# Queries and keys of the last six pairs: a token per partition and a transposing DMA in place of transposes on TensorE

## The chip, the cores and the metric

The kernel runs on one core of a Trainium2 chip. The metric is the device time of one execution in microseconds (us), the median over several runs. Engines: PE (TensorE, matrix products), DVE (VectorE), ACT (ScalarE), POOL (GpSimd) and SP (SyncE). Here SP only issues DMAs; POOL issues DMAs and also does elementwise work, in one order with them.

## The reference

Attention with a causal sliding window of 64 tokens, over 8 batches, 8 heads, 576 tokens and a head size of 64, followed by a two-layer network with a hard-swish between the layers.

```python
scores = scale * np.matmul(q, k.transpose(0, 1, 3, 2))
mask = (rel >= 0) & (rel < window)          # rel = query position - key position, window = 64
attn = softmax(np.where(mask, scores, -1e9))
attn_out = np.matmul(attn, v)
x = attn_out.transpose(0, 2, 1, 3).reshape(4608, 512)
h = x @ w_in                                # 512 -> 2048
out = (h * np.clip(h + 3.0, 0.0, 6.0) / 6.0) @ w_out
```

Inputs and output are float32 in DRAM; the kernel computes in bf16 with float32 sums.

## The kernel before

**Pairs.** The unit of attention is a pair: two heads of one batch, on partitions 0 to 63 and 64 to 127. There are 32 pairs, t = 4b + g (batch b, pair g of the batch). Pairs 0 to 7 have paths of their own at the start; from pair 8 on, `group(t, n)` (L781) is called once for each pair.

**What a group holds.** In the order in which the instructions are issued: P.V of pair t (`pv`, L421); the turning of pair t + 2 (`turn`, L289: 9 pieces x 2 heads x 2 for queries and keys = 36 transposes of 64x64 on PE, into the two PSUM banks `tk` and `tq`); the scores of pair t + 1 (`s_first` L309, `s_rest` L323) and behind them the softmax weights (`weights`: exponentials on ACT, L332 and L336, then three multiplications with the window's 0/1 mask on POOL, L341 and L344); the division by the row sums (`pv_out`, on DVE); the copy of the turned keys from PSUM to `KT` on DVE (`turned(t + 2, 0)`, L296); the turning of the output into `xT` (`x_`, L465: two or three transposing DMAs on SP); two units of the two-layer network (`weave(2)`); the copy of the turned queries to `QT` on ACT (`turned(t + 2, 1)`, L296); and the remaining units of the network that this group is due (`weave(n - 2)`).

**The network.** A block is 512 tokens. A first-layer unit is four matmuls 128x128x512 into `hT` (L513), then L525 on ACT and L526 on DVE make `gT`; a second-layer unit is four matmuls into `acc` (L550), and after sixteen of them ACT copies (L556) and SP stores (L558). Units wait in the queue `moe` and are woven between the attention's steps.

**Order.** Every engine works in the order of issue (the order is written out by hand). An engine that waits holds up all that stands behind it on that engine; between engines there are only the waits on data and on buffers.

**Loads.** POOL issues them, and they turn float32 into bf16 on the way. `load_qk(b, n, first)` (L124, L128) loads n pairs with one DMA for the keys and one for the queries: 64 partitions, on each of them 9 consecutive tokens of a head in one run of 2304 bytes. Token 9p + r stands on partition p, so the 9 pieces of a head are transposed one by one, and the copies L296 put the tokens back in order. After groups 8 to 27 the last loop (L906 to L931) issues the loads of the next batch: from batch 3 on pairs 0 and 1 after its first group, V after the second, and after the third the shifted copy of V (`shift`, L167 and L168, on SP) and pairs 2 and 3.

**Buffers.** `KT` and `QT` are rings of four, indexed t % 4; keys have 64 zero columns in front. Scores read the keys of a window with a step of two (`keys`, L301).

Of the kernel before, what the change touches and what calls it, by code (L numbers as in the profile page):

```python
# [11 lines left out]
BF16 = mybir.dt.bfloat16  # L12
# [13 lines left out]
P = 128  # L26
D = 64
W = 64
R = 6
VC = 72  # L30
RL = 9
# [6 lines left out]
def kernel(  # L38
# [9 lines left out]
    nc = tc.nc  # L48
    B, H, S, _ = q.shape
    DM, FF = moe_w_in.shape  # L50
    NT = B * S
    NG = H // 2
    SP = S // R
    NW = S // W
    NM = (S + P - 1) // P
# [9 lines left out]
    stage = ctx.enter_context(tc.tile_pool(name="stage", bufs=2))  # L65
# [13 lines left out]
    def ring(n, shape, dtype, name):  # L79
        return [consts.tile(shape, dtype, name=f"{name}{i}") for i in range(n)]  # L80
# [1 line left out]
    win16 = consts.tile([P, NG, FF], BF16, name="win16")  # L82
    wout16 = consts.tile([P, NFC, DM], BF16, name="wout16")
    xT = consts.tile([P, NG, XR], BF16, name="xT")
    KT = ring(4, [P, W + S], BF16, "KT")
    QT = ring(4, [P, S], BF16, "QT")
    QZ = ring(4, [P, 2, W], BF16, "QZ")
    Vflat = ring(4, [P, NM * H * VC], BF16, "V")
    Vn, Vs = ([t[:].rearrange("p (m h c) -> p m h c", m=NM, h=H) for t in Vflat[i::2]] for i in range(2))
# [5 lines left out]
    Pw = [t[:].rearrange("p h m a w -> p (h m a w)").rearrange("p (h c m r w) -> p h c m r w", h=2, c=2, m=2, r=2) for t in Pz]  # L95
    P0 = ring(4, [D, 2, 2, W], BF16, "P0")
    halves = (slice(0, D), slice(D, P))


    def load_pair_0():  # L100
# [23 lines left out]
    def load_qk(b, n=NG, first=0):  # L124
        t = staged[b] if first else stage.tile([P, H, RL * D], BF16, name="qk9", tag="qk")
        hs = slice(2 * first, 2 * (first + n))
        for z, src in enumerate((k, q)):
            nc.gpsimd.dma_start(  # L128
                out=t[halves[z], hs], in_=src[b, hs].rearrange("h (p r) d -> p h (r d)", r=RL)
            )  # L130
        return t

    def load_early_v():
        for m in range(NM):
            n = min(P, S - m * P)
            nc.gpsimd.dma_start(
                out=Vn[0][:n, m, :, 0:D], in_=v[0, :, m * P : m * P + n, :].rearrange("h s d -> s h d"),
            )
# [49 lines left out]
    first = consts.tile([P, 2, W], BF16, name="first")  # L188
# [29 lines left out]
    def transposed_heads(pool, src, g):  # L218

        tp = pool.tile([P, R, SP], BF16, name="tp", tag="bk")  # L220
        for r in range(R):
            for h in range(2):
                nc.tensor.transpose(
                    out=tp[h * D : (h + 1) * D, r, :],
                    in_=src[:, 2 * g + h, r * D : (r + 1) * D], identity=ident[:SP, :SP],
                )
        return tp

    def t_q(t):
        b, g = divmod(t, NG)  # L230
        tp = transposed_heads(ps_h, staged[b][0], g)
        nc.scalar.copy(
            out=QT[t][:].rearrange("q (p r) -> q p r", r=R), in_=tp[:].rearrange("q r p -> q p r"),
        )

    def padded(t, move=nc.vector.tensor_copy):
        for h in range(2):
            move(out=QZ[t][halves[h], h], in_=QT[t][halves[h], S - W : S])

    def t_k(t):  # L240
        b, g = divmod(t, NG)
        tp = transposed_heads(ps_acc, staged[b][1], g)
        nc.vector.tensor_copy(
            out=KT[t % 4][:, W:].rearrange("q (p r) -> q p r", r=R),
            in_=tp[:].rearrange("q r p -> q p r"),
        )

    def s_early(t):

        kt, qt = KT[t], QT[t]  # L250
        sc = [ps_t.tile([P, NM - 1, 2, W], F32, name="sc", tag="bk") for _ in range(2)]
# [42 lines left out]

    def turned(t, z, on_vector=False):
        (nc.scalar.copy if z and not on_vector else nc.vector.tensor_copy)(  # L296
            out=(QT[t % 4][:] if z else KT[t % 4][:, W:]).rearrange("q (p r) -> q p r", r=RL),
            in_=hosts[t][z][:, 0:S].rearrange("q (r p) -> q p r", p=W),
        )

    def keys(t, h, k0, r):  # L301
        return KT[t % 4][halves[h], W + k0 + r : W + k0 + P : 2]

    def s_first(t, host):

        s = [x[0:D, 6 * P : 8 * P].bitcast(F32).rearrange("p (r w) -> p r w", w=W) for x in hosts[host]]
        for r in range(2):
            for h in range(2):
                nc.tensor.matmul(  # L309
                    s[h][:, r], lhsT=keys(t, h, 0, r), rhs=QT[t % 4][halves[h], 0:W], start=True, stop=True,  # L310
                )
        return s

    def s_rest(t):

        ss = [ps_t.tile([P, 2, 2, 2, W], F32, name="s", tag="bk") for _ in range(2)]
        for c in range(2):
            for m in range(2):
                for r in range(2):
                    for h in range(2):  # L320
                        for i in range(2):
                            w = 4 * m + 2 * i + 1 + c
                            nc.tensor.matmul(  # L323
                                ss[h][halves[i], c, m, r], lhsT=keys(t, h, W * (w - 1), r),
                                rhs=QT[t % 4][halves[h], w * W : (w + 1) * W], start=True, stop=True,
                            )
        return ss

# [271 lines left out]
    def weave(n):  # L600
        for _ in range(min(n, len(moe))):
            moe.popleft()()
# [18 lines left out]
    def s_max(t, fm):  # L621
        kt, qt, pw, p0 = KT[t % 4], QT[t % 4], Pw[t % 4], P0[t % 4]
        for w in range(S // W):
            k0 = W * max(w - 1, 0)
            sc = ps_t.tile([P, 2, P], F32, name="sm", tag="bk")
            se = fb.tile([P, 2, P], F32, name="se", tag="fs")
            for h in range(2):
                nc.tensor.matmul(
                    sc[0:W, 0], lhsT=qt[halves[h], w * W : (w + 1) * W],
                    rhs=kt[halves[h], W + k0 : W + k0 + P], start=True, stop=True,  # L630
                )
                nc.vector.tensor_tensor(
                    out=se[0:W, h], in0=sc[0:W, 0], in1=fm[0:W, min(w, 1)], op=ADD,
                )
            mx = fb.tile([P, 2], F32, name="mx")
            nc.vector.reduce_max(out=mx[0:W], in_=se[0:W], axis=mybir.AxisListType.X)
            nc.vector.tensor_tensor(
                out=se[0:W], in0=se[0:W], in1=mx[0:W].unsqueeze(2).to_broadcast([W, 2, P]), op=SUB,
            )
            pe = work.tile([P, 2, P], BF16, name="pe", tag="e0")  # L640
            nc.scalar.activation(out=pe[0:W], in_=se[0:W], func=EXP, scale=scale)
            c, j = (w - 1) % 2, (w - 1) // 2
            part = halves[j % 2 if w else 0]
            tp = ps_t.tile([P, 2, 2, W], BF16, name="pt", tag="bk")
            for h in range(2):
                for r in range(2):
                    nc.tensor.transpose(
                        out=tp[part, h, r], in_=pe[0:W, h, r:P:2], identity=ident[0:W, 0:W]
                    )
            nc.vector.tensor_copy(out=pw[part, :, c, j // 2] if w else p0[:], in_=tp[part])  # L650
# [36 lines left out]
    T = B * NG  # L687

    def warm(pool, n, cols=TB):
# [5 lines left out]
    staged = {}  # L695
# [6 lines left out]
        out=ident[:], in_=ident[:], pattern=[[-1, P]], compare_op=mybir.AluOpType.not_equal,  # L702
# [4 lines left out]
    window()  # L707
    for t in KT:
        nc.vector.memset(t[:, 0:W], 0.0)
# [21 lines left out]
    warm(ps_h, 4, W)  # L731
    t_k(0)
    t_q(0)
    padded(0)
    t_k(1)
# [45 lines left out]
    def group(t, n):  # L781

        if t >= 2 * NG:
            pv(t)
        if t + 2 < T:
            turn(t + 2)
        if t + 1 < T:
            host = t + 2
            opened(host)
            s = s_first(t + 1, host)  # L790
            weights(t + 1, s, s_rest(t + 1))
        if t >= 2 * NG:
            pv_out(t)
        if t + 2 < T:
            turned(t + 2, 0)
        if t >= 2 * NG:
            x_(t)
        weave(2)
        if t + 2 < T:
            turned(t + 2, 1)  # L800
        weave(n - 2)

    def turn_two(t):
# [14 lines left out]
    n = NG  # L818
# [12 lines left out]
    for t in range(n, n + 4):  # L831
        if t < n + 3:
            turn(t + 1)
        s = s_first(t, min(t + 1, n + 3))
# [71 lines left out]
    for t in range(2 * NG, T):  # L906
        b, g = divmod(t, NG)
        if g == 0 and b > 2:
            queue_block(b - 1, lead=4 if b == 3 else 2)
            if b == 3:  # L910
                arrange(2, (
                    -1, -2, 0, 1, 2, 3, -3, 4, 5, -4, 6, 7, 8, -5, 9, -6, 10, 11, 12, 13, -7,
                    14, 15, -9, -10, -8, -11, -12,
                ))
        group(t, shares[g] if b == 2 else -(-len(moe) // (NG - g)))
        if b == 2:
            if g == 0:
                load_v(3)
            if g == 1:
                shift(3)  # L920
            if g > 0:
                load_qk(3, 1, g)
        elif b + 1 < B:
            if g == 0:
                staged[b + 1] = load_qk(b + 1, 1)
                load_qk(b + 1, 1, 1)
            if g == 1:
                load_v(b + 1)
            if g == 2:
                shift(b + 1)  # L930
                load_qk(b + 1, 2, 2)  # L931
    late[0] = 2
    queue_last(NTB - 2)
    flag = flagged()
# [35 lines left out]
```

## Time and profile before

| what | value |
|---|---|
| median of 3 runs | 315.24 us (315.19 to 315.67) |
| profiled execution, its own time | 316.28 us |
| span of its instructions | 314.6 us |
| mean granted PE clock | 0.995 |
| DMA, mean | 114 GB/s |

The span runs from the first to the last instruction on the core; the rest of the execution's time lies around it. A page cuts the span into 40 slices of some 7.9 us, with the busy share of each engine in tenths. The chain of waits is followed back from the last instruction: at each step to what released it. In a timeline a row has its start (us from the start of the span), its length, the engine, the line, and the instruction; rows of SP and the DMA rows of POOL are the issue of a DMA and not its transfer. A row that stands for several instructions ends with their count.

### The profile page before, as it was taken

The page shows a single profiled execution, that of the slowest core. Times are in us where ns is not written, and L with a number is a line of the kernel's source. Part 1 is how long each engine was busy: PE and PEld are TensorE (multiplying, and loading weights), DVE is VectorE, ACT ScalarE, POOL GpSimd, SP SyncE. Part 2 cuts the span into 40 slices and gives each one's busy share as a digit, 9 for nine tenths or more (in the row PEclk, how much of TensorE's full clock was granted, in tenths as well). Part 3 has the DMA queues.
Part 4 walks back from the last instruction along what each step waited for, and adds up shares of the span by engine and source line. Part 5 has one row for each costly group of instructions (what it writes and reads, how often), then busy time and mean ns, then how long its engine had stood idle before and what let it go on. Part 6 is the DMA issues. An engine that isn't in the chain of part 4 may idle for free.

```text
span 314.6 us, 10707 instructions
## 1 busy us (share of the span) xinstructions
PE 299.5 (95%) x4565; PEld 151.0 (48%) x4608; DVE 180.4 (57%) x411; ACT 184.6 (59%) x350; POOL 131.3 (42%) x181
## 2 busy tenths in 40 slices
PE   7889989999999999999999999999999999999992
PEld 3454445555555554444555555555544444444440
DVE  7767647598547755773577447754776155344200
ACT  3838555877658656773677457754764266454410
POOL 8861404868887536653665366533330000000000
PEclk9999999999999999999999999999999999999998
DMA  8999995969996976697469744983021100100121
GB/s 155 167 205 200 198 192 123 220 119 100 205 144 102 144 167 114 76 132 188 84 83 139 169 109 79 131 193 88 19 56 52 69 33 0 70 34 33 36 82 60
DMA packets 57848, 35.96 MB, mean 114 GB/s; under 512 B 40128, under 2 KB 51904, under 8 KB 57792
## 3 DMA queue, kind: packets, MB, share of 16 engines
q0 software_dynamic: 35744, 18.52, 45.8%
q1 hardware_dynamic: 22048, 16.67, 21.0%
q8 instruction: 38, 0.62, 0.8%
q14 instruction: 18, 0.15, 0.1%
HBM read 37.62 MB, written 9.44 MB: 150 GB/s over the span
## 4 chain that ended last, share of the span: by engine, by line
PE 81%; DMA 9%; POOL 3%; DVE 3%; issue 2%; ACT 1%; POOLq 0%; ACTq 0%; DVEq 0%
PE acc L550 36%; PE hT L513 34%; DMA qk<-in_q_dram 7%; PE o L421 4%; PE s L323 3%; DMA V<-in_v_dram 2%; PE tk L289 2%; PE acco L550 1%; POOL qk L117 1%; PE tq L289 1%; DVE gT L526 1%; POOL qk L128 1%; POOL wout L179 1%; DVE opl L448 0%; DVE V L160 0%
## 5 line engine op out<-in xcount | busy, mean ns | idle before, releaser
L526 DVE SCALAR_TENSOR_TENSOR gT<-t,hT 128x512 bf16<-128x512 bf16 x141 | 95.7, 686 | 74.3 <-ACT t L525 73.2
L513 PE MATMUL hT<-xT,win 128*128 128x512 bf16 x548 | 131.5, 379 | 1.1 <-DVE gT L526 0.2
L550 PE MATMUL acc<-wout,gT 128*128 128x512 bf16 x522 | 126.7, 379 | 2.5 <-issue 1.1
L525 ACT ACTIVATE t<-hT,half_const 128x512 bf16<-128x512 f32 x141 | 95.6, 689 | 48.2 <-PE hT L513 46.3
L513 PEld LDWEIGHTS <-win 128*128 128x128 bf16 x576 | 55.3, 98 | 65.2 <-issue 0.4
L550 PEld LDWEIGHTS <-gT 128*128 128x128 bf16 x576 | 54.5, 98 | 64.2 <-issue 0.9
L344 POOL TENSOR_TENSOR Pz<-e,band 128x512 bf16<-128x512 bf16 x48 | 54.1, 1144 | 0.0
L341 POOL TENSOR_TENSOR P<-e,first 64x256 bf16<-64x256 bf16 x24 | 15.8, 660 | 74.4 <-ACT e L332 74.4
L556 ACT COPY osb<-acc 128x512 f32<-128x512 f32 x34 | 19.9, 586 | 42.0 <-PE acc L550 42.0
L336 ACT ACTIVATE e<-s 128x512 bf16<-128x512 f32 x56 | 30.1, 591 | 0.0
L296 DVE COPY KT<-tk 128x576 bf16<-128x576 bf16 x28 | 21.0, 749 | 6.9 <-ACT e L332 5.8
L147 POOL DMA_DIRECT2D V<-in_v_dram x22 | 18.0, 829 | 8.5 <-DMA wout<-in_moe_w_out_dram 5.6
L448 DVE TENSOR_TENSOR opl<-o,recs 128x256 bf16<-128x256 f32 x52 | 19.6, 419 | 0.5
L430 DVE TENSOR_REDUCE sums<-o 128x10 f32<-128x20 f32 x26 | 4.6, 175 | 23.9 <-PE o L421 23.8
L296 ACT COPY QT<-tq 128x576 bf16<-128x576 bf16 x27 | 17.2, 638 | 1.5 <-PE tq L289 1.5
L332 ACT ACTIVATE e<-tk 64x128 bf16<-64x128 f32 x28 | 7.6, 270 | 17.7 <-PE tq L309 17.7
L421 PEld LDWEIGHTS <-Pz 64*64 64x64 bf16 x1008 | 11.4, 108 | 10.7 <-issue 10.2
L289 PE MATMUL tk<-ident,qk 64*64 64x64 bf16 x504 | 14.3, 195 | 0.0
L289 PE MATMUL tq<-ident,qk 64*64 64x64 bf16 x504 | 14.0, 195 | 0.3 <-DMA qk<-in_q_dram 0.3
L128 POOL DMA_DIRECT2D qk<-in_k_dram x22 | 14.1, 640 | 0.3 <-issue 0.3
L323 PE MATMUL s<-QT,KT 64*64 64x64 bf16 x896 | 13.8, 194 | 0.0
L128 POOL DMA_DIRECT2D qk<-in_q_dram x22 | 13.8, 627 | 0.0
(106 smaller groups left out, 199.9 us busy)
## 6 DMA issues: line engine op xcount, KB each, us to landing
out_dram<-osb SPq DMA_DIRECT2D x36, 256.0 KB, 2.5
V<-in_v_dram POOLq DMA_DIRECT2D x16, 256.0 KB, 6.0
qk<-in_q_dram POOLq DMA_DIRECT2D x19, 144.0 KB, 4.5
qk<-in_k_dram POOLq DMA_DIRECT2D x19, 144.0 KB, 4.3
V<-V SPq DMA_DIRECT2D x6, 432.0 KB, 5.1
wout<-in_moe_w_out_dram POOLq DMA_DIRECT2D x2, 1024.0 KB, 17.4
qk<-in_k_dram POOLq DMA_DIRECT2D x6, 288.0 KB, 4.4
qk<-in_q_dram POOLq DMA_DIRECT2D x6, 288.0 KB, 5.6
```

The costliest lines, as they stand in the source:

```text
L128: nc.gpsimd.dma_start(out=t[halves[z], hs], in_=src[b, hs].rearrange("h (p r) d -> p h (r d)", r=RL))
L289: nc.tensor.transpose(out=hosts[t][z][halves[h], r * W : (r + 1) * W], in_=staged[b][halves[z], 2 * g + h, r * D : (r + 1) * D], identity= ...
L296: (nc.scalar.copy if z and not on_vector else nc.vector.tensor_copy)(out=(QT[t % 4][:] if z else KT[t % 4][:, W:]).rearrange("q (p r) -> q ...
L323: nc.tensor.matmul(ss[h][halves[i], c, m, r], lhsT=keys(t, h, W * (w - 1), r), rhs=QT[t % 4][halves[h], w * W : (w + 1) * W], start=True, ...
L336: nc.scalar.activation(out=e[:].rearrange("p c m r w -> p (c m r w)"), in_=ss[h][:].rearrange("p c m r w -> p (c m r w)"), func=EXP, scale ...
L344: muls[h].tensor_tensor(out=Pw[t % 4][:, h].rearrange("p c m r w -> p (c m) (r w)"), in0=e[:].rearrange("p c m r w -> p (c m) (r w)"), in1 ...
L421: nc.tensor.matmul(o[i][halves[c], c0 : c0 + D + 1], lhsT=p, rhs=vt[:, hh, v0 : v0 + D + 1], start=(r == 0), stop=(r == 1), skip_group_che ...
L513: nc.tensor.matmul(hT, lhsT=win16[:, g, fc * P : (fc + 1) * P], rhs=xT[:, g, t0 : t0 + TB], start=(g == 0), stop=(g == NG - 1),)
L525: nc.scalar.activation(out=t1[:], in_=hT, func=RELU, bias=half_const[:], scale=1.0 / 6.0)
L526: nc.vector.scalar_tensor_tensor(out=gT[:, fc, :], in0=t1[:], scalar=1.0, in1=hT, op0=MIN, op1=MULT)
L550: nc.tensor.matmul(acc, lhsT=gT[:, fc, ts * P : (ts + 1) * P], rhs=wout16[:, fc, :], start=(fc == 0), stop=(fc == NFC - 1),)
L556: nc.scalar.copy(out=osb[:], in_=acc)
```

## The change

For the pairs 26 to 31 (`by_rows`: the last two of batch 6 and all four of batch 7) the transposes on PE and the two copies out of PSUM fall away. Their loads bring one token per partition into a tile `rows` (a ring of four): four DMAs of 128 partitions with 4 runs of 256 bytes each (keys and queries of each head, tokens 0 to 511), and two of 64 partitions with 2 runs each (the last 64 tokens of both heads, keys on partitions 0 to 63 and queries on 64 to 127). Three groups ahead, at the end of the first two units of the network in group t - 3, SP issues three transposing DMAs that write keys and queries side by side into one tile `KQ`. `KQ` takes the place of `KT` and `QT`, which become views of it for the other pairs. The two PSUM banks `tk` and `tq` are still opened for every pair, as the first window's scores stand in them. The new function `load_pairs` also loads pair by pair where a DMA for two pairs stood before (pairs 2 and 3 of batches 4 and 5).

```diff
-    KT = ring(4, [P, W + S], BF16, "KT")
-    QT = ring(4, [P, S], BF16, "QT")
+    KQ = ring(4, [P, W + 2 * S], BF16, "KQ")
+    KT, QT = [t[:, 0 : W + S] for t in KQ], [t[:, W + S :] for t in KQ]
+    by_rows = range(B * NG - 6, B * NG)
...
+    rows = {}
...
+    def load_rows(t):
+
+        b, g = divmod(t, NG)
+        m = NM - 1
+        rows[t] = stage.tile([P, 2 * m + 1, 2, D], BF16, name="rows", tag="rows", bufs=4)
+        for z, src in enumerate((k, q)):
+            for h in range(2):
+                nc.gpsimd.dma_start(
+                    out=rows[t][:, z * m : (z + 1) * m, h],
+                    in_=src[b, 2 * g + h, 0 : m * P].rearrange("(m p) d -> p m d", p=P),
+                )
+            nc.gpsimd.dma_start(
+                out=rows[t][halves[z], 2 * m], in_=src[b, 2 * g : 2 * g + 2, m * P :].rearrange("h p d -> p h d")
+            )
+
+    def rows_turned(t):
+
+        m = NM - 1
+        src = rows.pop(t)[:].rearrange("p m h d -> p (m h d)")
+        for i, j, c in ((0, m, 0), (2 * m, 2 * m + 1, m * P), (m, 2 * m, (m + 1) * P)):
+            nc.sync.dma_start_transpose(
+                out=KQ[t % 4][:, c : c + (j - i) * P].rearrange("q (m p) -> q m p", p=P),
+                in_=src[:, i * P : j * P],
+            )
+
+    def load_pairs(b, n, first):
+        for g in range(first, first + n):
+            t = b * NG + g
+            if t in by_rows:
+                load_rows(t)
+            elif g:
+                load_qk(b, 1, g)
+            else:
+                staged[b] = load_qk(b, 1)
...
     def keys(t, h, k0, r):
+        if t in by_rows:
+            return KQ[t % 4][halves[h], k0 + r : k0 + P : 2]
         return KT[t % 4][halves[h], W + k0 + r : W + k0 + P : 2]
+
+    def queries(t, h, w):
+        if t in by_rows:
+            c = S if w == NW - 1 else S + W + w * W
+            return KQ[t % 4][halves[h], c : c + W]
+        return QT[t % 4][halves[h], w * W : (w + 1) * W]
...
-        if t + 2 < T:
+        turned_here = t + 2 < T and t + 2 not in by_rows
+        if turned_here:
             turn(t + 2)
...
         weave(2)
-        if t + 2 < T:
+        if turned_here:
             turned(t + 2, 1)
+        if t + 3 in by_rows:
+            rows_turned(t + 3)
         weave(n - 2)
...
             if g == 0:
-                staged[b + 1] = load_qk(b + 1, 1)
-                load_qk(b + 1, 1, 1)
+                load_pairs(b + 1, 2, 0)
             if g == 1:
                 load_v(b + 1)
             if g == 2:
                 shift(b + 1)
-                load_qk(b + 1, 2, 2)
+                load_pairs(b + 1, 2, 2)
```

More of the change, by code (lines that the diff above doesn't have):

```diff
@@ L232, in t_q @@
         nc.scalar.copy(
-            out=QT[t][:].rearrange("q (p r) -> q p r", r=R), in_=tp[:].rearrange("q r p -> q p r"),
+            out=QT[t].rearrange("q (p r) -> q p r", r=R), in_=tp[:].rearrange("q r p -> q p r"),
         )
@@ L296, in turned @@
         (nc.scalar.copy if z and not on_vector else nc.vector.tensor_copy)(
-            out=(QT[t % 4][:] if z else KT[t % 4][:, W:]).rearrange("q (p r) -> q p r", r=RL),
+            out=(QT[t % 4] if z else KT[t % 4][:, W:]).rearrange("q (p r) -> q p r", r=RL),
             in_=hosts[t][z][:, 0:S].rearrange("q (r p) -> q p r", p=W),
@@ L309, in s_first @@
                 nc.tensor.matmul(
-                    s[h][:, r], lhsT=keys(t, h, 0, r), rhs=QT[t % 4][halves[h], 0:W], start=True, stop=True,
+                    s[h][:, r], lhsT=keys(t, h, 0, r), rhs=queries(t, h, 0), start=True, stop=True,
                 )
@@ L324, in s_rest @@
                                 ss[h][halves[i], c, m, r], lhsT=keys(t, h, W * (w - 1), r),
-                                rhs=QT[t % 4][halves[h], w * W : (w + 1) * W], start=True, stop=True,
+                                rhs=queries(t, h, w), start=True, stop=True,
                             )
@@ L798, in group @@
         weave(2)
-        if t + 2 < T:
+        if turned_here:
             turned(t + 2, 1)
+        if t + 3 in by_rows:
+            rows_turned(t + 3)
         weave(n - 2)
```

## The prediction

> **What bounds the kernel now.** I read the page first (busy shares, slices, the chain of waits), then the chain in order of time, then the timelines of PE, POOL and SP where the last six pairs (26 to 31) are prepared.
>
> ```profile
> PE 299.5 (95%) x4565; PEld 151.0 (48%) x4608; DVE 180.4 (57%) x411; ACT 184.6 (59%) x350; POOL 131.3 (42%) x181
> PE   7889989999999999999999999999999999999992
> POOL 8861404868887536653665366533330000000000
> PE 81%; DMA 9%; POOL 3%; DVE 3%; issue 2%; ACT 1%; POOLq 0%; ACTq 0%; DVEq 0%
> ```
>
> PE is busy nine tenths or more in every slice from the seventh to the last but one, and 81% of the chain runs through it. So in the stretch that the change touches (170 to 240 us) a microsecond taken out of PE's program is a microsecond of the end, and a microsecond in which PE waits costs one. POOL averages 42%, but what counts is where its work stands between two deadlines of PE.
>
> The chain's rows for the P.V products of pairs 24, 26 and 28 give these deadlines; one group (one pair's attention with its share of the MoE) lasts about 8.1 us (198.21 to 214.45 is two).
>
> ```profile
> 181.98 0.44 PE o L421 x40
> ...
> 198.21 0.45 PE o L421 x40
> ...
> 214.45 0.45 PE o L421 x40
> ```
>
> **What is removed.** For each of the six pairs 36 64x64 transposes on PE (L289) and two copies out of PSUM (L296). PE's timeline shows what the transposes take when they run packed, from the first one to the first score matmul behind them:
>
> ```profile
> 206.59 0.19 PE L289 MATMUL tk<-ident,qk 64*64 64x64 bf16 x1
> ...
> 206.93 0.20 PE L309 MATMUL tk<-QT,KT 64*64 64x64 bf16 x1
> ...
> 214.73 0.19 PE L289 MATMUL tk<-ident,qk 64*64 64x64 bf16 x1
> ...
> 215.06 0.19 PE L309 MATMUL tk<-QT,KT 64*64 64x64 bf16 x1
> ```
>
> That is 0.34 and 0.33 us, not 36 times the 0.19 us of a single row, as the matmuls overlap. Six pairs make 6 x 0.335 = **2.0 us** off PE, in groups 24 to 29 (group t turns pair t + 2). The two copies lie on engines with room:
>
> ```profile
> L296 DVE COPY KT<-tk 128x576 bf16<-128x576 bf16 x28 | 21.0, 749 | 6.9 <-ACT e L332 5.8
> L296 ACT COPY QT<-tq 128x576 bf16<-128x576 bf16 x27 | 17.2, 638 | 1.5 <-PE tq L289 1.5
> ```
>
> They free 6 x 0.75 us of DVE and 6 x 0.64 us of ACT. Both are below 60% busy while PE is full, so I count them as nothing; no row shows PE waiting on them here.
>
> **What is added on SP.** Three transposing DMAs for each pair, issued behind the pair's output transposes of the same group. The nearest rows are the output transposes (L465), one of the same 128x4x128 shape:
>
> ```profile
> L465 SPq DMA_TRANSPOSE xT<-opl x28: 1097/1232/2177, 68.6 to 241.6; - x28
> L465 SPq DMA_TRANSPOSE xT<-opg x24: 1202/1221/2439, 70.0 to 242.9; - x24
> ...
> xT<-opl SPq DMA_TRANSPOSE x28, 2.8
> ...
> 184.20 1.22 SPq L465 DMA_TRANSPOSE xT<-opl x1
> 185.47 1.21 SPq L465 DMA_TRANSPOSE xT<-opg x1
> 193.17 1.51 SPq L465 DMA_TRANSPOSE xT<-opl x1
> ```
>
> At 1.23 us each they hold SP for 3.7 us a pair. Between 186.7 and 193.2 SP has nothing to issue, so they fit in a group beside 2.4 us of output transposes and about a microsecond of stores. They land 2.8 us after issue, and pair t is wanted by its first scores in group t - 1, two groups (some 15 us) after group t - 3, where they stand: cost nothing. If each took the 2.4 us of the slowest row, five a group would be 12 us against 8; that is a rival below.
>
> The Trainium skill (VectorE: DVE Perf Modes, section "The three transpose paths") speaks against this part: it lists 1309 ns for a 128x128 DMA transpose against 390 ns on TensorE. Nine blocks would by it be 11.8 us of transposing a pair, more than a group. The trace disagrees with such a serial price: four blocks issue in 1.23 us and land in 2.8, and 36 small transposes cost PE 0.34 us.
>
> **What is added on POOL, the part that decides.** Loads of pairs 26 and 27 (after group 22), 28 and 29 (after 24), 30 and 31 (after 26). Each such point now issues a burst of **12** DMAs, where it had 2, 4 and 2: for each pair four of 128 partitions x 4 runs of 256 B and two of 64 partitions x 2 runs. (Two earlier points, for batches 4 and 5, go from 2 to 4 DMAs; 1.3 us more inside a POOL idle of 4 us, nothing.) All stand on POOL between two sets of mask multiplications (L341, L344), which P.V of the next pair waits for:
>
> ```profile
> 170.07 0.68 POOL L128 DMA_DIRECT2D qk<-in_k_dram  x1
> ...
> 175.36 0.66 POOL L341 TENSOR_TENSOR P<-e,first 64x256 bf16<-64x256 bf16 x1 [4.00 <-ACT e L332]
> ...
> 183.49 0.66 POOL L341 TENSOR_TENSOR P<-e,first 64x256 bf16<-64x256 bf16 x1 [5.24 <-ACT e L332]
> ...
> 186.33 0.64 POOL L128 DMA_DIRECT2D qk<-in_k_dram  x1
> ...
> 194.74 2.43 POOL L147 DMA_DIRECT2D V<-in_v_dram  x3
> ...
> 199.71 0.66 POOL L341 TENSOR_TENSOR P<-e,first 64x256 bf16<-64x256 bf16 x1 [2.54 <-ACT e L332]
> ...
> 202.55 0.68 POOL L128 DMA_DIRECT2D qk<-in_k_dram  x1
> ...
> 207.84 0.66 POOL L341 TENSOR_TENSOR P<-e,first 64x256 bf16<-64x256 bf16 x1 [3.99 <-ACT e L332]
> ```
>
> One set takes 186.33 - 183.49 = 2.84 us. What a DMA of 512 runs costs POOL has two near rows, and one on each side:
>
> ```profile
> 6.54 4.23 POOL L136 DMA_DIRECT2D V<-in_v_dram  x5
> 10.72 1.54 POOL L173 DMA_DIRECT2D win<-in_moe_w_in_dram  x2
> ...
> L136 POOL DMA_DIRECT2D V<-in_v_dram x5: 722/896/908, 6.5 to 10.0; - x5
> ...
> L128 POOL DMA_DIRECT2D qk<-in_q_dram x22 | 13.8, 627 | 0.0
> ```
>
> L173 issues 128 partitions x 4 runs, the new shape: 1.54 us for two, 0.77 each, about 0.75 from start to start. The fifth early V load (64 partitions x 8 runs of 256 B) is the 722 ns one, and its 1024-run neighbours take 0.90. The 128-run loads of L128 take 0.63, some 0.61 from start to start. I take 0.745 for the large and 0.61 for the small ones: a burst of D = 8 x 0.745 + 4 x 0.61 = **8.4 us**. Bounds: all at 0.61, 7.3 us; the large ones at the 1024-run loads' start spacing of (10.72 - 6.54 - 0.72) / 4 = 0.865, 9.4 us.
>
> Now the deadlines, with PE's own gain of 0.33 us a group taken off:
> - First burst, from 170.07: the set for pair 24 ends at 170.07 + D + 2.84 = 181.3, P.V wants it at 181.98. Free while D < 9.07.
> - Second, from 186.33 - 0.33 = 186.00: set 26 ends at 197.2, wanted at 198.21 - 0.67 = 197.54. Free while D < 8.70. POOL then has V's three loads (2.42 us) and set 27 (ready to start at 198.7, but POOL comes free only at 199.7), which ends at 194.10 + D = 202.5 and is still early for its own P.V.
> - Third, from there: set 28 ends at 196.94 + 2D = 213.74, wanted at 214.45 - 1.33 = 213.12. **PE waits 0.6 us** in front of pair 28's P.V, and I add 0.15 for the hand-over from POOL to PE, an estimate.
>
> After pair 28 POOL has only one set a group. The stall is 2D - 16.18 from D = 8.1 on, and 3D - 25.25 from 9.07 on, where the first burst is late too and pushes the others.
>
> A second thing could lengthen a burst. POOL's DMAs take turns on eight completion counters, so that the ninth waits until the first has landed. The trace shows it where large weight loads stand eight places ahead of V's:
>
> ```profile
> 13.70 0.76 POOL L173 DMA_DIRECT2D win<-in_moe_w_in_dram  x1
> ...
> 18.00 0.90 POOL L179 DMA_DIRECT2D wout<-in_moe_w_out_dram  x1
> ...
> 25.63 0.88 POOL L147 DMA_DIRECT2D V<-in_v_dram  x1 [2.47 <-DMA win<-in_moe_w_in_dram]
> 32.10 1.87 POOL L147 DMA_DIRECT2D V<-in_v_dram  x2 [5.58 <-DMA wout<-in_moe_w_out_dram]
> ...
> DMA to landing us min/median/max: 4.6/5.3/5.9
> ```
>
> The last row is that of the early V loads, the only ones of 256-byte runs. The ninth DMA of a burst is due 6 x 0.745 + 2 x 0.61 = 5.7 us after the first. With 5.3 us it finds its counter free; with 5.9 it waits 0.2. I count 0.
>
> **The sum.** -2.0 + 0.6 + 0.15 = -1.2 us on the profiled execution's 316.28 us (span 314.6 us). The part is absolute and takes place inside the span, so I take it off the median of the runs, 315.24: **314.0 us**.
>
> **The rivals.**
> 1. *POOL keeps up.* D below 8.1 us, if the runs' number hardly matters (0.63 for 128 and 0.72 for 512 speak for it, L173's 0.77 against). No wait: -2.0, 313.2 us. Chance 0.13.
> 2. *A draw.* D of 8.7 to 9.25, the large loads at 0.78 to 0.85: stall 1.2 to 2.5 with hand-over 1.4 to 2.65, so -0.6 to +0.6, about 315.2 us. Chance 0.20.
> 3. *Slower: the mask multiplications come late behind each burst.* From D = 9.25 on, by 1024-run prices or by a counter that comes back late. At 9.4: 3 x 9.4 - 25.25 = 2.95, +0.15 - 2.0 = +1.1, 316.3 us. If the first loads land only after 6.7 us, D is again 9.4; each further microsecond of landing costs three. For it: the new loads meet V's and the shift's traffic, and up to six times as many DMAs take turns on the counters. Against: near rows for issue and landing both lie below. Chance 0.27.
> 4. *SP falls behind.* At the slowest rows (2.4 us) five transposes a group make 12 us in 7.8. The backlog of 4.4 us a group eats the 15 us of lead after three to four groups, and the last two or three pairs' scores wait 4 us each: +10 - 2, some 323 us. Only single rows reach 2.4, so 0.07. The serial price of the Trainium skill quoted above, 11.8 us a pair, would make this the outcome; the landing of 2.8 us for four blocks speaks against it.
>
> **How the numbers follow.** The forecast's own case is D of 8.1 to 8.7 (313.4 to 314.6 us), chance 0.33. About 0.2% (0.63 us) can be told from no change: faster is 0.33 + 0.13 = 0.46, the same 0.20, slower 0.34. The range is 313.1 (all of the gain, nothing paid) to 316.8 us (D up to 9.55); beyond it lie rival 4 and the longest bursts.
>
> **What would show it.** Right: no tk or tq transposes after group 23; PE's gap between P.V and the first score gone, 0.33 us a group; bursts of 12 on POOL of about 8.4 us; an idle of some 0.7 us of PE (or its weight loads) put down to POOL's mask multiplications in front of pair 28's P.V, none in front of 24 and 26; transposes on SP landing in about 3 us and no PE wait on them. Wrong: idle in POOL between the DMAs of a burst (counters), single issues at 0.85 us or more, PE waits in front of the P.V of pairs 24 and 26, score matmuls that wait for a DMA, or SP without pause from 176 us on.

## The result, and the profile after

The changed kernel takes 317.58 us (median of 22 runs, 316.44 to 320.80) where the kernel before takes 315.84 us (22 runs beside it, 315.12 to 318.17). The ratio is 1.0064, with a 95% interval of 1.0045 to 1.0082: it is **slower, by 1.4 to 2.6 us**. Forecast were 314.0 us and a gain. Ratios, here and below, leave out executions more than 1.5% above the fastest of the same kernel: none of these 44, one each in e8 and e13, seven of twelve in e12. The profiled execution has a span of 317.1 us against 314.6; it took 318.90 us, 1.3 above the median of the 22.

From the page of the changed kernel, busy shares and PE's slices:

```profile
PE 302.5 (95%) x4392; PEld 149.6 (47%) x4392; DVE 176.7 (56%) x405; ACT 181.7 (57%) x344; POOL 154.0 (49%) x213
PE   7889999999999999999999979996999999999994
```

Before, no slice of PE after the sixth was under nine tenths except the last. Now there are two holes, a 7 and a 6, in the slices around 185 and 217 us. How much they hold is read from one stretch, 160 to 240 us (columns: length, busy time of PE, weight loads, DVE, ACT, POOL, granted clock, DMA share, GB/s). Before:

```profile
160.00:240.00 80.00, 79.26 (x1323) 40.05 (x1332) 49.94 (x109) 51.69 (x98) 37.64 (x43) 1.00 0.55 103
```

and after:

```profile
160.00:240.00 80.00, 74.60 (x1058) 36.37 (x1057) 43.30 (x98) 45.72 (x88) 57.48 (x71) 1.00 1.19 122
```

PE sits idle for 5.4 us in place of 0.7. The extra 4.7 us less the 2.0 us that the transposes took is +2.7 us; the span grew by 2.5. So the trace has room for the full gain and for a loss of over twice its size. Whom PE waited for, in the changed kernel (total, times, longest, in us):

```profile
PE o L466 <- DMA V<-V: 2.7, 2, 1.7
PE hT L558 <- DMA xT<-opg: 2.0, 1, 2.0
...
PE tk L354 <- DMA KQ<-rows: 0.5, 1, 0.5
```

None of these rows is POOL. All are DMAs that **SP** issued: the shifted copy of V, the output transposes, the new transposes. PE's timeline shows where they stand (the two waits for V are in front of pair 28's P.V, of which a few matmuls ran at 215.62 and 217.58):

```profile
183.78 0.81 PE L558 MATMUL hT<-xT,win 128*128 128x512 bf16 x3
186.55 1.25 PE L558 MATMUL hT<-xT,win 128*128 128x512 bf16 x5 [1.96 <-DMA xT<-opg]
...
208.17 0.19 PE L354 MATMUL tk<-KQ 64*64 64x64 bf16 x1 [0.53 <-DMA KQ<-rows]
...
215.62 0.22 PE L466 MATMUL o<-V,Pz 64*64 64x65 bf16 x2
217.58 0.19 PE L466 MATMUL o<-V,Pz 64*64 64x65 bf16 x1 [1.74 <-DMA V<-V]
218.74 0.42 PE L466 MATMUL o<-V,Pz 64*64 64x65 bf16 x29 [0.97 <-DMA V<-V]
```

That is 2.0 us in front of the first network unit that needs the last slice of `xT`, 0.5 in front of pair 28's scores, and 2.9 us from 215.84 to 218.74 in front of its P.V. The chain names the transfers that ended these waits and one more that started late scores (start, length):

```profile
179.11 7.39 DMA xT<-opg
...
200.87 7.26 DMA KQ<-rows
...
210.88 7.82 DMA V<-V
```

SP's timeline shows what stood in line (a row is the issue, with its length; the shift of V is two copies, a large one of 432 KB and a small one of 72 KB):

```profile
198.15 4.35 SPq L155 DMA_TRANSPOSE KQ<-rows  x3
202.60 1.21 SPq L510 DMA_TRANSPOSE xT<-opl  x1
203.86 1.72 SPq L510 DMA_TRANSPOSE xT<-opg  x1
205.74 3.81 SPq L155 DMA_TRANSPOSE KQ<-rows  x3
209.65 0.53 SPq L603 DMA_DIRECT2D out_dram<-osb  x1
210.28 0.54 SPq L204 DMA_DIRECT2D V<-V  x1
210.88 2.03 SPq L205 DMA_DIRECT2D V<-V  x1
```

The shift of V is issued at 210.28; in the trace before the same shift was issued at 206.61:

```profile
179.07 1.23 SPq L465 DMA_TRANSPOSE xT<-opg  x1
...
206.61 0.54 SPq L167 DMA_DIRECT2D V<-V  x1
```

It comes 3.7 us later. The program as a whole was 1.1 us later by then (P.V of pair 26 starts at 199.34 in place of 198.21); the rest comes from the three new transposes just ahead of it, 3.81 us of issue. Then its small copy, the one that ended the wait, takes 7.8 us to land. It takes both to hurt, by an estimate: issued where it was but landing in the 4.4 us of before, the small copy would be there at 215.28, before PE came to it; landing as late but issued only 1.1 us after 207.20, the place of before, it would be there at some 216.2, for a wait of 0.3 us.

Landings as a whole, in 165 to 216 us (KB each, median us to landing). Before:

```profile
q0 software_dynamic: 5931, 2.84, 44.8%
q1 hardware_dynamic: 5337, 3.79, 27.2%
...
V<-V SPq DMA_DIRECT2D x2, 72.0 KB, 4.4
xT<-opl SPq DMA_TRANSPOSE x8, 2.7
xT<-opg SPq DMA_TRANSPOSE x6, 2.4
```

After:

```profile
q0 software_dynamic: 17644, 2.67, 104.4%
q1 hardware_dynamic: 9485, 4.46, 53.7%
...
KQ<-rows SPq DMA_TRANSPOSE x13, 5.7
V<-V SPq DMA_DIRECT2D x2, 72.0 KB, 7.8
xT<-opl SPq DMA_TRANSPOSE x8, 5.1
xT<-opg SPq DMA_TRANSPOSE x6, 5.4
```

The first two rows of each are the queue of POOL's loads and that of SP: packets, MB, and the time that the packets took as a share of 16 engines. POOL's loads bring no more bytes, but in three times the packets and over twice their time. SP's queue has 1.8 times the packets, with the new transposes, and twice their time, so that a single packet of SP took some 11% longer (an estimate from these rows). The output transposes, which the change does not touch, land in 5 us where they took 2.5.

### The profile page after: what moved, and what is told of

It is laid out like the page before. It is cut to its first block, busy times and chain, and to the rows that moved or that the text cites. A ratio compares the mean times of both kernels' runs of the same rounds, so it can differ in the third digit from the quotient of the medians.

```text
span 317.1 us, 10385 instructions
## 1 busy us (share of the span) xinstructions
PE 302.5 (95%) x4392; PEld 149.6 (47%) x4392; DVE 176.7 (56%) x405; ACT 181.7 (57%) x344; POOL 154.0 (49%) x213
## 4 chain that ended last, share of the span: by engine, by line
PE 80%; DMA 9%; DVE 4%; ACT 2%; POOL 2%; issue 1%; SPq 1%; POOLq 0%; ACTq 0%
PE hT L558 36%; PE acc L595 32%; PE o L466 3%; PE s L368 3%; DMA V<-V 2%; DMA xT<-opg 2%; PE acco L595 2%; DMA KQ<-rows 2%; DMA V<-in_v_dram 2%; PE tk L326 2%; DVE gT L571 1%; POOL qk L119 1%; ACT t L570 1%; PE hTo L558 1%; DVE opl L493 1%
## 5 line engine op out<-in xcount | busy, mean ns | idle before, releaser
L558 PE MATMUL hT<-xT,win 128*128 128x512 bf16 x564 | 133.0, 379 | 2.2 <-DMA xT<-opg 2.0
L595 PE MATMUL acc<-wout,gT 128*128 128x512 bf16 x544 | 129.2, 379 | 0.0
L333 DVE COPY KQ<-tk 128x576 bf16<-128x576 bf16 x22 | 16.5, 750 | 5.6 <-ACT e L377 4.5
L466 PE MATMUL o<-V,Pz 64*64 64x65 bf16 x936 | 13.8, 195 | 2.7 <-DMA V<-V 2.7
L368 PE MATMUL s<-KQ 64*64 64x64 bf16 x896 | 14.5, 195 | 0.2
L333 ACT COPY KQ<-tq 128x576 bf16<-128x576 bf16 x21 | 13.4, 639 | 1.5 <-PE tq L326 1.5
L130 POOL DMA_DIRECT2D qk<-in_k_dram x20 | 12.6, 631 | 0.3 <-issue 0.3
L130 POOL DMA_DIRECT2D qk<-in_q_dram x20 | 12.5, 623 | 0.0
L368 PEld LDWEIGHTS <-KQ 64*64 64x64 bf16 x896 | 11.1, 107 | 0.5 <-issue 0.4
```

Source lines behind the costliest of these rows:

```text
L130: nc.gpsimd.dma_start(out=t[halves[z], hs], in_=src[b, hs].rearrange("h (p r) d -> p h (r d)", r=RL))
L368: nc.tensor.matmul(ss[h][halves[i], c, m, r], lhsT=keys(t, h, W * (w - 1), r), rhs=queries(t, h, w), start=True, stop=True,)
L466: nc.tensor.matmul(o[i][halves[c], c0 : c0 + D + 1], lhsT=p, rhs=vt[:, hh, v0 : v0 + D + 1], start=(r == 0), stop=(r == 1), skip_group_che ...
L558: nc.tensor.matmul(hT, lhsT=win16[:, g, fc * P : (fc + 1) * P], rhs=xT[:, g, t0 : t0 + TB], start=(g == 0), stop=(g == NG - 1),)
L595: nc.tensor.matmul(acc, lhsT=gT[:, fc, ts * P : (ts + 1) * P], rhs=wout16[:, fc, :], start=(fc == 0), stop=(fc == NFC - 1),)
```

## The experiments

All ratios are against the kernel before, run beside it on the same chip, with a 95% interval. Ratios from different chips are compared below; the kernel before took 315.64 to 316.12 us on them.

| run | ratio | interval |
|---|---|---|
| changed kernel | 1.0064 | 1.0045 to 1.0082 |
| e1 loads only | 0.9972 | 0.9944 to 1.0000 |
| e2 transposes only | 0.9944 | 0.9915 to 0.9973 |
| e3 neither | 0.9953 | 0.9927 to 0.9980 |
| e4 long runs | 0.9989 | 0.9955 to 1.0023 |
| e5 spread | 1.0068 | 1.0039 to 1.0096 |
| e6 transposes late in the group | 1.0073 | 1.0044 to 1.0102 |
| e7 clear of the batch boundary | 1.0096 | 1.0062 to 1.0130 |
| e8 unlinked | 1.0033 | 1.0004 to 1.0061 |
| e9 spread, V early | 1.0005 | 0.9979 to 1.0030 |
| e10 spread, V early, more lead | 0.9959 | 0.9933 to 0.9985 |
| e11 spread, more lead | 1.0101 | 1.0076 to 1.0127 |
| e12 as e10, ten pairs | 1.0100 | 1.0066 to 1.0133 |
| e13 kernel before, V early | 1.0004 | 0.9985 to 1.0023 |
| e14 changed kernel, V early | 1.0075 | 1.0050 to 1.0101 |

**Which part: e1 to e4.** The first four take the change apart. e1 leaves the new transposes out:

```diff
-        if t + 3 in by_rows:
-            rows_turned(t + 3)
```

> The 18 new transposing DMAs are left out (scores of the last six pairs use what an earlier pair left in KQ); the new loads stay. Theory A (the loads' 2304 small packets a pair, against 256 before, hold up everything that SP sends): the output transposes and the shift of V still land after 7 us in 175 to 215 us, PE still waits 3 us or more for them, about +1 to +1.5 us against before. Theory B (the new transposes, standing on SP's queue ahead of the output transposes and the shift, hold them up): landings back at 2.7 and 5 us, no PE wait, -2.0 us. Theory D (transposes and small-run loads in flight together stop each other, so either alone is harmless): few stops are left, as only the output transposes meet the loads, -1 to -2 us.

e2 keeps the transposes, on a constant tile, and loads as before:

```diff
-            if t in by_rows:
-                load_rows(t)
-            elif g:
+            if g:
...
-        src = rows.pop(t)[:].rearrange("p m h d -> p (m h d)")
+        src = still[:].rearrange("p m h d -> p (m h d)")
```

> The loads are those of before (into a tile that no one reads), PE's transposes of the six pairs are left out, and the 18 new transposing DMAs read a constant tile. Theory A: -2.0 us, landings of before. Theory B: output transposes and the shift land late as in the changed kernel, 0 to +1.7 us. Theory D: -1 to -2 us, as the large-run loads are in flight for a shorter time.

e3 has the edit of e1 and the first edit of e2: the six pairs are not turned at all.

> Loads of before, no turning at all for the six pairs (scores use what an earlier pair left): the gain by itself. All theories: -2.0 us (6 x 0.335 us of PE), 313.2 us; if the transposes on PE were hidden anyway, 0.

e4 is the changed kernel with four tokens of a head in one run:

```diff
-                    out=rows[t][:, z * m : (z + 1) * m, h],
-                    in_=src[b, 2 * g + h, 0 : m * P].rearrange("(m p) d -> p m d", p=P),
+                    out=rows[t][:, (2 * z + h) * m * D : (2 * z + h + 1) * m * D],
+                    in_=src[b, 2 * g + h, 0 : m * P].rearrange("(p m) d -> p (m d)", m=m),
```

> The changed kernel, but the 24 large loads bring four consecutive tokens per partition in one run of 1024 bytes (tokens stand in another order, so scores are of other pairs of tokens): the same number of DMAs, bytes and transposes, 128 packets a load where it had 512. Theory A: landings on SP near those of before, -1 to -2 us. Theory B: as the changed kernel, +1.7 us. Theory D: in between, fewer stops as the loads are in flight for a shorter time. POOL's bursts go from 8.7 to about 7.5 us in any case.

e3 gives the gain by itself: 0.9953, which is -1.5 us (-0.6 to -2.3) and agrees with the 2.0 us counted. The transposes alone (e2) cost nothing measurable on top of it, the small loads alone (e1) 0.2% by the point values, less than the intervals can tell. **Together** they cost 1.1% over e3. So theories A and B fall as single causes, and of the theories written down D is left: the loss needs the two kinds of transfer in flight together. That they slow each other in a way of their own is not shown by it (see the last section). e4 bears on why: with a quarter of the packets in the large loads 0.75% of the 1.1% go away, against the changed kernel. That is size and not proof, as long runs also make POOL's bursts shorter (the first takes 6.8 us in its trace, 169.37 to 176.18).

**Where it reaches PE: e5 to e7.** I supposed that only two near deadlines matter and moved the work away from them: e5 loads one pair after each group,

```diff
             if t in by_rows:
-                load_rows(t)
+                continue
...
+        if t + 4 in by_rows:
+            load_rows(t + 4)
```

> The changed kernel, but one pair's loads (six DMAs) after each of groups 22 to 27 in place of twelve after 22, 24 and 26. New theory S (late landings cost only where PE has a near deadline: the output transposes of a batch's last pair, 23 and 27, and the shift of V before it): bursts of 4.3 us leave gaps, but loads now also run in groups 23 and 27, so about half the loss is left: 0 to +1 us against before. Theory D (total time in which loads and transposes are in flight together): as the changed kernel, +1.5 us. If POOL's long bursts alone were the trouble: -1.5 us.

e6 issues the new transposes behind `weave(n - 2)`, at the end of the group,

> The changed kernel, but the three new transposing DMAs stand at the end of their group, behind its stores, some 5 us after the output transposes. Theory S: the output transposes of 23 land before the new ones start, PE's 2.0 us wait for them shrinks below 1 us; the shift still comes behind the transposes of pair 28: -0.5 to +0.5 us against before. Theory D: as the changed kernel, +1.5 us, since as many are in flight beside the loads.

and e7 moves both away from groups 23 and 27 (with the `continue` of e5; the `rows_turned` of the changed kernel goes):

```diff
+        for i in {20: (26,), 21: (27,), 24: (28, 29), 25: (30,), 26: (31,)}.get(t, ()):
+            load_rows(i)
...
+        for i in {22: (26,), 24: (27,), 25: (28,), 26: (29, 30), 28: (31,)}.get(t, ()):
+            rows_turned(i)
```

> The changed kernel, with loads and new transposes kept away from the two batch boundaries: loads of 26 after group 20, 27 after 21, 28 and 29 after 24, 30 after 25, 31 after 26; transposes of 26 in group 22, 27 in 24, 28 in 25, 29 and 30 in 26, 31 in 28 (none in groups 23 and 27). Theory S: no PE wait for xT in group 24, at most 1 us before pair 28: -1 to -1.5 us against before. Theory D: as many meet, +1 us or more.

All three failed: 1.0068, 1.0073, 1.0096. But their waits moved. e5 waits for V (1.4 us) and for the new transposes (1.2) in place of `xT`; its profiled execution, 316.35 us where the median is 318.11, shows only part of the loss. e6 has no wait for `xT` left and waits for the new transposes instead (and 0.3 us for V); e7 waits for nothing but the shift of V (and 0.8 us for POOL), whose issue stood behind six transposes, put there by e7's own edit. e6:

```profile
PE tk L354 <- DMA KQ<-rows: 2.0, 1, 2.0
```

e7:

```profile
PE o L466 <- DMA V<-V: 3.3, 1, 3.3
...
PE o L466 <- POOL Pz L389: 0.8, 1, 0.8
```

Each removed wait uncovered the next one, mostly on SP's queue. In e6 and e7 a lower clock behind the wait added to the loss (last section).

**Does SP wait for the loads? e8.** It is the changed kernel, with the transposes reading the constant tile of e2 while the small loads run on, unread.

> Loads and new transposes as in the changed kernel, but the transposes read a constant tile in place of the loaded one, so that SP waits for no load (scores of the last six pairs come from that constant). Theory D (small-run loads and transposes in flight together slow each other, whatever waits for what): as the changed kernel, +1.5 to +2 us against before. Theory W (SP stands at the new transposes until the loads have landed, and so holds up stores, shift and output transposes): the loss is gone, -1 to -1.5 us, as with the loads alone or the transposes alone.

1.0033 lies between. Without any link between load and transpose a loss is left (1.0004 to 1.0061, against 0.9944 for the same transposes beside the old loads), so the loss needs both transfers in flight, but no link between them. Measured from e3, the gain by itself, e8 has 0.8% of the changed kernel's 1.1%. SP's standing still for loads (W) can be the rest, but the intervals overlap, and the changed kernel's trace has little of it (SP's waits at the new transposes for their loads):

```profile
SPq L155 <- DMA rows<-in_q_dram: 2.7, 4, 1.1
```

2.7 us in four waits. e8's profiled execution waits 3.0 us for the new transposes; it took 320.25 us where the median is 317.46.

**All deadlines at once: e9 to e11.** e9 is e5 with V's loads and its shift a group earlier for batches 6 and 7:

```diff
-            if g == 1:
+            if g == (0 if b > 4 else 1):
                 load_v(b + 1)
-            if g == 2:
+            if g == (1 if b > 4 else 2):
                 shift(b + 1)
+            if g == 2:
                 load_pairs(b + 1, 2, 2)
```

> One pair's loads after each of groups 22 to 27, and V's loads and its shift for batches 6 and 7 one group earlier. If the late shift is what costs: no PE wait for V before pairs 24 and 28, 1.4 us less than with the spread loads alone, 0 to +0.8 us against before. If other late landings take its place: still +1.5 us or more.

e10 adds one group of lead for loads and transposes (the edit is against the changed kernel; `t + 5` takes the place of e5's `t + 4`):

```diff
-        if t + 3 in by_rows:
-            rows_turned(t + 3)
+        if t + 4 in by_rows:
+            rows_turned(t + 4)
...
+        if t + 5 in by_rows:
+            load_rows(t + 5)
```

> As the kernel with early V, and loads and transposes of the six pairs one more group ahead (loads after groups 21 to 26, transposes in groups 22 to 27). Only waits for the output transposes of pairs 23 and 27 can be left: -1.2 to 0 us against before if late landings at near deadlines are all that costs; +1.5 us or more if the slowing of the DMAs reaches PE in another way.

e11 is e10 with V at its old place.

> Spread loads and transposes one group further ahead, as in the kernel that came out ahead, but V and its shift at their old places. If the missing lead of the turned keys and queries was the loss: -1 us against before. If both it and the shift matter: 0 to +1.5 us, with a PE wait for V before pair 24 or 28. DMA landings stay at 5 us in either case.

These make a square over spread loads: neither 1.0068, V early 1.0005, lead 1.0101, both 0.9959. e10 is the one form of the change that is **faster than the kernel before**, by 1.3 us. Its landings in 165 to 216 us are nearly as slow as those of the changed kernel:

```profile
KQ<-rows SPq DMA_TRANSPOSE x16, 4.8
...
xT<-opl SPq DMA_TRANSPOSE x8, 5.7
...
xT<-opg SPq DMA_TRANSPOSE x6, 5.1
```

and still PE is idle for only 0.2 us of the stretch (in its profiled execution, 312.92 us, the quickest of its twelve; the median is 314.69):

```profile
160.00:240.00 80.00, 79.79 (x1119) 38.92 (x1118) 46.51 (x107) 47.83 (x91) 54.49 (x67) 1.00 1.25 122
```

The landings are much the same; what waits for them differs. Without the early shift, lead alone does not help (1.0101 beside 1.0068, with intervals that overlap), and PE waits in e11 for what it waited for in the changed kernel:

```profile
PE o L466 <- DMA V<-V: 2.7, 3, 1.6
PE hT L558 <- DMA xT<-opg: 1.8, 1, 1.8
```

**Its limit, and two controls: e12 to e14.** e12 extends e10 to ten pairs.

> The scheme of the kernel that came out ahead (spread loads, a group more of lead, V early), for the last ten pairs in place of six (V early from batch 5 on). If landings of 5 us stay hidden: 10 x 0.335 = 3.4 us of PE, -2 to -2.6 us against before. If the DMA engines are at their end: no better than the six pairs, -0.5 us or slower than before.

It is slower than before, by how much is uncertain: 1.0100 rests on five of the twelve executions, and the median of all twelve is 322.13 us beside 316.03. The profiled one (325.13 us, the longest) waits 7.3 us for the output transposes, once. e13 gives the kernel before the early V.

> The kernel before, with V's loads and shift for batches 6 and 7 one group earlier. If the shift was in time before (no PE wait for V in its trace): 0, within 0.2 us. If the early place is a gain of its own: -1 us or more.

1.0004: no gain of its own that can be told, so the shift was in time before, and its delay is a price of the change. e14 gives it to the changed kernel, bursts of twelve kept.

> The changed kernel, with V's loads and shift for batches 6 and 7 one group earlier, bursts of twelve and the lead of three groups kept. If the shift behind the new transposes is the larger part of the loss: -0.5 to +0.5 us against before, with no PE wait for V; if late output transposes and late keys take its place: +1 us or more. POOL's second burst now has V's loads ahead of it (10.9 us), so set 26 may come 1.5 to 2 us late.

1.0075: no wait for V or `xT` is left, but POOL takes their place, as V's loads now share a burst:

```profile
PE o L466 <- POOL Pz L389: 3.1, 2, 2.3
```

From 186.14 to 198.44 POOL issues loads, 12.3 us in place of 8.7 (1.4 us of it waiting). So in these runs spread loads, early V and lead gain only together; bursts of twelve with early V and more lead were not run.

## Why the prediction was wrong, point by point

**The gain: right.** The transposes are gone, and e3 shows a gain of 1.5 us (0.6 to 2.3) that agrees with 2.0; e10 keeps 1.3 of it.

**POOL's bursts: right.** The changed kernel's timeline has the three bursts, from the first load to the first multiplication behind them:

```profile
169.41 1.58 POOL L142 DMA_DIRECT2D rows<-in_k_dram  x2
...
177.84 0.79 POOL L386 TENSOR_TENSOR P<-e,first 64x256 bf16<-64x256 bf16 x1
...
185.34 1.55 POOL L142 DMA_DIRECT2D rows<-in_k_dram  x2
...
194.03 0.68 POOL L386 TENSOR_TENSOR P<-e,first 64x256 bf16<-64x256 bf16 x1
...
203.43 1.56 POOL L142 DMA_DIRECT2D rows<-in_k_dram  x2
...
209.50 0.60 POOL L146 DMA_DIRECT2D rows<-in_k_dram  x1 [0.28 <-DMA rows<-in_k_dram]
...
212.21 0.71 POOL L386 TENSOR_TENSOR P<-e,first 64x256 bf16<-64x256 bf16 x1
```

8.43, 8.69 and 8.78 us for a forecast of 8.4; the counters, put at nothing, cost 0.3 us in the third. The forecast wait of 0.6 us in front of pair 28 does not show here, as PE was already later than that for other reasons. It does show in e1, where the loads run without the new transposes: one wait of 0.3 us, in front of that P.V.

```profile
PE o L466 <- POOL Pz L389: 0.3, 1, 0.3
```

In e14 a longer burst makes PE wait for 3.1 us. So the part that the prediction called the deciding one was sound, and was not what decided.

**"They land 2.8 us after issue ... cost nothing": wrong, and this is the step that failed.** It put the new transposes' cost at nothing with a landing taken from a trace in which few small packets ran beside them. With three times the packets of POOL's loads in the same stretch, and the new transposes there too, the transposes on SP landed in medians of 5.1 to 5.7 us and the shift of V in 7.0 and 7.8, and PE waited 5.2 us in all for DMAs that SP had issued. The text had asked what traffic does to the ninth counter of POOL, and never what POOL's traffic does to SP.

**"They fit in a group", "some 15 us": both too roomy.** SP's rows, added up, cover 46.3 of the 49 us from 176 to 225, where they covered 25.1 before: the sign that the prediction names, SP without pause from 176 us on, came true, and so did a score matmul that waits for a DMA. A full SP is no loss by itself (47.1 us in e2), but what is issued behind the new transposes leaves later. And the new transposes stand late in their group: those of pair 28 are issued from 198.15 on, and its scores were due at 207.64 (208.17 less the wait of 0.53), 9.5 us later. The last of the three, issued at 200.87, had 6.8 us and took 7.26.

**The lead was reckoned for the wrong transfer.** Two groups of lead for the new transposes were counted, but not what stands behind them on SP. The shift of V was not mentioned as a deadline at all, though it is issued once a batch just ahead of the P.V that needs it; e9 against e5 prices its place, with that of V's loads, at 0.6%, e10 against e11 at 1.4%. The last output transpose of a batch was issued at 179.07 before and landed some 2.4 us later; the first network unit that reads it stands in the row that begins at 184.76, so there was room for about 3 us more:

```profile
184.76 1.89 PE L513 MATMUL hT<-xT,win 128*128 128x512 bf16 x8
```

In the changed kernel it was issued at 179.11 and took 7.39.

**The rivals.** "SP falls behind" named the right queue with the wrong mechanism: the new transposes issue in 1.2 us (median; one took 2.7), as taken, not in 2.4, and e2 shows that they alone are harmless. The slower rival by POOL did not happen. The 317.58 us lie above the 316.8 at which the range ends, as the range held only POOL's unknowns.

**What stays open.** Why landings grow when small-run loads and transposes are both in flight was not isolated. e1, e2, e4 and e8 show that the loss takes both, and e4 that fewer packets hurt less. A plain sum of work on the 16 DMA engines is a rival that no run rules out.

## What to carry to other kernels

When an edit multiplies the packets of one DMA queue, take the landing times of every other queue in that stretch as unknown, and list for each of its transfers who waits and how much is to spare, the rare ones (once a batch) first. A slow landing is free with lead and dear without: with landings of about 5 us in both cases the change cost 0.6% or gained 0.4%, by where V's shift, the loads and the transposes stood. Give lead to all of them at once, since a single repair only uncovered the next wait.

## What the runs showed of the hardware

Each kind of transfer delayed the output transposes a little by itself. The larger ones (`opl`) landed in medians of 2.7 to 2.8 us with neither (before, e3), 3.5 with the new transposes alone (e2), 4.0 with the new loads alone (e1) and 5.1 with both (165 to 216 us). The two delays, 0.8 and 1.3 us, simply added would make 4.8. The smaller ones (`opg`, six in the stretch) are less orderly: 2.4 and 4.1, 4.9, 3.5 and 5.4. The new loads of 64 KB landed in 3.4 to 3.7 us in e1 and in 5.6 in the changed kernel. The packet times of POOL's and SP's queues, as shares of the 16 engines, add up to 72% before, 103% in e2, 124% in e1 and 158% in the changed kernel. So the landings come near to adding up; what does not add up is the cost, as PE waits only once a landing passes its deadline.

And a hole in PE's work cost more than its length where it was longer than 2 us: in e14, after PE stood still for most of 198 to 202 us, the granted clock fell, and the next matmuls ran slower.

```profile
198.00:202.00 4.00, 0.87 (x53) 0.75 (x56) 0.59 (x1) 0.00 (x0) 3.34 (x4) 0.91 1.47 178
202.00:206.00 4.00, 4.00 (x54) 1.85 (x45) 2.28 (x7) 2.71 (x6) 3.17 (x4) 0.67 1.12 110
206.00:210.00 4.00, 4.00 (x20) 1.80 (x19) 2.40 (x4) 2.43 (x5) 4.00 (x7) 1.00 1.19 181
```

The clock was 0.67 of full speed in the 4 us behind the hole, then 1.00 again. All five traces in which PE, from 90 us on, waited 2.04 us or more at once show this: e6 (2.04), e14 (2.29), e8 (2.67), e7 (3.32) and e12 (7.29). Each has a stretch of 2 us at 0.50 within 4 us of the wait's end, and 1.00 again 6 us after it. In e6, e7, e8 and e14 that is some 1.7 us of lost work, an estimate from the clock in stretches of 2 us. After waits of up to 1.96 us (the changed kernel, e4, e5, e9, e11) every such stretch shows 1.00. So the holes of the changed kernel, the second of which is broken by a matmul at 217.58, cost only their length, and part of what e6, e7, e8 and e14 lost in their profiled executions is this. Whether the length alone decides it is not shown.
